# Loading and transposing the first 256 tokens of k and q in another way: sliding-window attention with a gated feed-forward block on one core

## The chip, the core and the metric

The kernel runs on one core of one Trainium2 chip. The time is the device time of one execution in microseconds (us). A core has five engines that run their own instruction streams and wait for each other by semaphores: TensorE (PE in the profile: matmuls and transposes; PEld is its weight load), VectorE (DVE), ScalarE (ACT), GpSimd (POOL) and SyncE (SP). Data moves between the device memory and the on-chip memory (SBUF) by DMA. A DMA is put into a queue by ScalarE or SyncE (the profile calls these queues hardware_dynamic: q10 is ScalarE's, q1 SyncE's) or by GpSimd (software_dynamic, q0). Only DMAs that GpSimd issues change the type on the way here, float32 to bfloat16. TensorE writes into PSUM, eight banks of 2 KB per partition, and VectorE or ScalarE brings results from there to SBUF (an eviction).

## The reference

```python
batch, n_heads, seq, head_dim = (8, 8, 576, 64)
...
scores = scale * np.matmul(q, k.transpose(0, 1, 3, 2))      # scale = 1/8
pos = np.arange(S)
rel = pos[:, None] - pos[None, :]
mask = (rel >= 0) & (rel < 64)
scores = np.where(mask, scores, -1000000000.0)
...
attn = attn / (np.sum(attn, axis=-1, keepdims=True) + 1e-09)   # after the exponential
return np.matmul(attn, v)
...
x = attn_out.transpose(0, 2, 1, 3).reshape(4608, 512)
g = x @ w_gate                                   # 512 x 1536
silu = g * (1.0 / (1.0 + np.exp(-g)))
val = x @ w_val
return silu * val @ w_out                        # 1536 x 512
```

All inputs and the output are float32. q, k and v are [8, 8, 576, 64] (batch, head, token, dimension). Every token sees itself and the 63 before it in its batch.

## The kernel before

The 4608 tokens are cut into 36 chunks of 128 for the attention and 9 blocks of 512 for the feed-forward part. Everything is computed in bfloat16 with float32 sums.

**Attention of a chunk n.** `Sa` takes two PSUM banks, `Sbias` writes the mask into them by two matmuls (identity by `nmask`), `Sb` adds the scores of the 8 heads (24 small matmuls) and ScalarE makes the exponentials into `pt` (two activations, L450). For these the chunk's k and q must lie transposed, the dimension on partitions, in `kT` and `qT`. `AVs` multiplies `pt` by v (`va`, with a column of ones that gives the sum); for n > 0 it reads for half of the rows a copy `vs` in which the last 64 tokens of the chunk before and the first 64 of this one stand together. `shift(n, r, eng)` writes one half of such a copy, on GpSimd or VectorE. `AVn` divides by the sum (a reciprocal and a multiplication on VectorE) and writes `xb`. `X` transposes `xb` into `xT` by TensorE and an eviction.

**Feed-forward.** `F(c, fs, lo, hi)` multiplies the tokens lo to hi of block c by the columns `fs` of both weight matrices (L815), applies tanh on ScalarE and two operations on VectorE, and writes `hT`. `O` multiplies `hT` by the output weights (L850), and ScalarE stores the rows.

**Order.** `build` lists all operations by hand in one sequence; each engine runs those that are its own in that order, and a small graph turns reads and writes of buffers into semaphore waits. An engine that waits holds up everything behind it in its stream. GpSimd is in this way also a queue: a load that it issues can't go out before a `shift` that stands ahead of it. PSUM banks are taken from a written list (`rot`) in the opening and, from `self.lru = True` on, by the one whose last use lies furthest back in the sequence.

**The opening before the change.** `first_loads` brings k of the first 256 tokens as float32 by two hardware DMAs (SyncE, ScalarE), four heads each, on 64 partitions each; a partition holds four tokens of each of the four heads, in rows of 1 KB. They land in `fk`, which borrows space from `hT`. `first_T` casts it on VectorE into `ck` (which borrows from `ost`), then 8 full transposes in two banks and two evictions fill `kT` for chunks 0 and 1. q of these tokens comes by a software DMA (`load2(0, "q")`, two tokens of a head per row) which casts on the way; `T2` transposes it with 16 matmuls of 64 columns in two banks and two evictions. The second 256 tokens of k and q (`load2(1, ...)`) go the same way as this q. `loads` writes the order of GpSimd's queue: the three loads of q and k, then the identity and the mask (selects on GpSimd), then v of four chunks, then the weights in pieces of 256 columns with the shifts between them. `T2w` is a form of `T2` with one bank and one wide eviction, used from the third pair of chunks on. `warm` runs matmuls on zeros into a bank that nobody reads.

Of the kernel before, what the change touches and what calls it, by code (L numbers as in the profile page):

```python
# [9 lines left out]
T = B * S  # L10
# [143 lines left out]
class _Kernel:  # L154
# [17 lines left out]
    def alloc(self):  # L172
# [35 lines left out]
        f4 = lambda a: a.bitcast(F32).rearrange("p (h j d) -> p h j d", h=4, j=4)  # L208
        self.fk = f4(hT[1][:, 0:2048])
        self.fkk = [("hT", 1, f) for f in range(4)]  # L210
        c4 = lambda t: t[:, :].bitcast(BF).rearrange("p (j h d) -> p j h d", j=4, h=4)
        self.ck = c4(self.ost[0])
# [8 lines left out]
    def touched(self, j):  # L221
        k = ("ps", j)
        return max([o.i for o in self.g.readers.get(k, ())] + [o.i for o in self.g.writers.get(k, ())])
# [135 lines left out]
    def T2(self, st, x, engs):  # L359
        g = self.g  # L360
        src = (self.ks2 if x == "k" else self.qs2)[st % 2]
        dst = self.kT if x == "k" else self.qT
        z0 = (2 * st) % self.NZ
        for cc in range(2):
            bank, bk = self.bank("a")
            tb = bank[:, 0:256].bitcast(BF).rearrange("p (c j t) -> p c j t", c=2, j=2)

            def pe(e, cc=cc, tb=tb):
                for c in range(2):
                    for j in range(2):  # L370
                        for p in range(2):
                            r = e.transpose(tb[64 * p:64 * p + 64, c, j, :], src[:, 4 * cc + 2 * c + p, j, :], self.ident[:, :])
                return r

            g.op("pe", pe, reads=["ident", ("s2", x, st % 2, 0), ("s2", x, st % 2, 1)], writes=[bk])
            d = dst[:, 2 * cc:2 * cc + 2, 128 * z0:128 * z0 + 256].rearrange("p c (t j) -> p c t j", j=2)
            a = tb.rearrange("p c j t -> p c t j")
            self.copy(engs[cc], d, a, [bk], [(x + "T", z, cc) for z in (z0, z0 + 1)])

    def T2w(self, st, x):  # L380
# [12 lines left out]

        self.g.op("pe", pe, reads=["ident", ("s2", x, st % 2, 0), ("s2", x, st % 2, 1)], writes=[bk])
        d = dst[:, :, 128 * z0:128 * z0 + 256].rearrange("p c (t j) -> p c t j", j=2)
        a = tb.rearrange("p c j t -> p c t j")
        self.copy("act", d, a, [bk], [(x + "T", z, b) for z in (z0, z0 + 1) for b in range(2)])
# [366 lines left out]
    def first_T(self, engs):  # L764
        g = self.g
        d = self.ck.rearrange("p j h d -> p h j d")
        self.copy("dve", d, self.fk, [("f", 0), ("f", 1)] + self.fkk, [("ost", 0), ("osth", 0)])
        for c in range(2):
            bank, bk = self.bank("a")
            tb = bank[:, 0:256].bitcast(BF).rearrange("p (j t) -> p j t", j=4)  # L770

            def pe(e, c=c, tb=tb):
                for j in range(4):
                    r = e.transpose(tb[:, j, :], self.ck[:, j, 2 * c:2 * c + 2, :], self.ident[:, :])
                return r

            g.op("pe", pe, reads=["ident", ("ost", 0), ("osth", 0)], writes=[bk])
            d = self.kT[:, c:4:2, 0:256].rearrange("p g (t j) -> p g t j", j=4)
            a = tb.rearrange("p j (g t) -> p g t j", g=2)
            self.copy(engs[c], d, a, [bk], [("kT", m, c) for m in (0, 1)])  # L780

    def warm(self, count, n=512, j=None):
        if j is None:
            ids, i = self.rot["a"]
            j = ids[i % len(ids)]
        bank, bk = self.ps[j], ("ps", j)
# [140 lines left out]
    def build(self):  # L927
        F, S, AV, X, T2, O = self.F, self.S, self.AV, self.X, self.T2, self.O
        self.loads()
        self.banks("a", [4, 5, 6, 7, 0, 1, 2, 3, 4, 5, 0, 1, 2, 3, 4, 5, 6, 7, 0, 1, 2, 3, 4, 5, 6, 7, 6, 7])  # L930
        self.warm(72, n=80)
        self.first_T(("dve", "act"))
        s0 = self.Sa(0)
        T2(0, "q", ("act", "dve"))
        self.Sbias(s0)
        self.warm(2)
# [3 lines left out]
        T2(1, "k", ("dve", "act"))  # L940
        T2(1, "q", ("dve", "act"))
        self.early_loads()
        s2, s3 = self.Sa(2), self.Sa(3)
        a0, a1, a2, a3 = self.AVa(0), self.AVa(1), self.AVa(2), self.AVa(3)
        self.AVs(a0)
        self.shift(1, 0, "dve")
        self.AVn(a0)
        self.Sbias(s2)
# [7 lines left out]
        self.warm(1, j=2)  # L956
        self.AVs(a2)
        self.AVn(a2)
        self.AVs(a3)
# [6 lines left out]
        self.banks("a", [4, 5, 6, 7])  # L966
# [3 lines left out]
        self.lru = True  # L970
# [3 lines left out]
        self.T2w(2, "k")  # L974
        self.T2w(2, "q")
# [7 lines left out]
        self.T2w(3, "k")  # L983
        self.T2w(3, "q")
        X(4, "act")
        X(5, "act")
        F(0, (11,))
# [10 lines left out]
        self.T2w(4, "k")  # L998
        self.T2w(4, "q")
# [109 lines left out]
```

## Time and profile before

| | us |
|---|---|
| median of 3 runs | 329.23 (329.14 to 330.06) |
| profiled execution, whole | 330.35 |
| its span, first to last instruction | 328.6 |
| first F matmul (L815) starts | 17.00 |
| TensorE busy in the span | 320.9 (98%) |
| VectorE, ScalarE, GpSimd busy | 214.2, 126.7, 107.2 |

How the times of the opening lie, from the timeline (start and length in us):

| start | length | engine | what |
|---|---|---|---|
| 0.81 | 0.75 | SP | issue of k's first load, lands 5.5 after |
| 0.82 | 0.71 | ACT | issue of k's second load, lands 4.1 after |
| 1.30 | 4.44 | PE | 72 warm-up matmuls |
| 1.32 | 1.01 | POOL | issue of q, first 256 tokens, lands 5.8 after |
| 2.33 | 0.88 | POOL | issue of k, second 256 tokens, lands 6.2 after |
| 3.20 | 0.90 | POOL | issue of q, second 256 tokens, lands 6.9 after |
| 4.16 | 1.13 | POOL | identity and mask, three selects |
| 5.38 | 3.91 | POOL | issue of four loads of v, each lands 5.0 to 5.5 after |
| 6.36 | 0.69 | DVE | cast of k |
| 9.26 | 0.78 | POOL | issue of the first gate weights, land 5.9 after |
| 10.01 | 0.78 | POOL | issue of the first value weights, land 6.5 after |
| 9.20 | 0.4 | PE | scores of chunk 0 |
| 12.79 | 1.3 | PE | scores of chunk 2 |
| 16.14 | 0.9 | PE | A·V of chunks 2 and 3 |

The granted clock of TensorE was 1.00 over the whole span. "Busy" of an engine is the time in which it runs an instruction; TensorE's instructions overlap, so a busy TensorE isn't one at its peak. The landing of a DMA is counted from the start of its issue.

### The profile page before, as it was taken

The page shows a single profiled execution, that of the slowest core. Times are in us where ns is not written, and L with a number is a line of the kernel's source. Part 1 is how long each engine was busy: PE and PEld are TensorE (multiplying, and loading weights), DVE is VectorE, ACT ScalarE, POOL GpSimd, SP SyncE. Part 2 cuts the span into 40 slices and gives each one's busy share as a digit, 9 for nine tenths or more (in the row PEclk, how much of TensorE's full clock was granted, in tenths as well). Part 3 has the DMA queues.
Part 4 walks back from the last instruction along what each step waited for, and adds up shares of the span by engine and source line. Part 5 has one row for each costly group of instructions (what it writes and reads, how often), then busy time and mean ns, then how long its engine had stood idle before and what let it go on. Part 6 is the DMA issues. An engine that isn't in the chain of part 4 may idle for free.

```text
span 328.6 us, 8039 instructions
## 1 busy us (share of the span) xinstructions
PE 320.9 (98%) x3447; PEld 165.7 (50%) x3447; DVE 214.2 (65%) x399; ACT 126.7 (39%) x222; POOL 107.2 (33%) x137
## 2 busy tenths in 40 slices
PE   6899999999999999999999989999999999999996
PEld 6584556475545454545444444545454544444444
DVE  4576954898666767685858586767676767555510
ACT  2645575445433333343324242424242331332221
POOL 8999930582060615050424224241310010000000
PEclk9999999999999999999999999999999999999999
DMA  9999999999999999999796959496939252000012
GB/s 140 178 194 186 196 182 176 154 169 151 132 100 139 127 120 123 135 118 140 116 142 95 153 95 169 87 150 95 158 69 112 67 66 64 34 32 32 34 64 96
DMA packets 157347, 39.33 MB, mean 120 GB/s; under 512 B 144384, under 2 KB 152832, under 8 KB 157312
## 3 DMA queue, kind: packets, MB, share of 16 engines
q0 software_dynamic: 109008, 18.62, 77.9%
q1 hardware_dynamic: 42848, 10.63, 24.5%
q10 hardware_dynamic: 5456, 9.57, 8.7%
q8 instruction: 27, 0.44, 0.6%
q14 instruction: 8, 0.07, 0.1%
HBM read 37.75 MB, written 9.44 MB: 144 GB/s over the span
## 4 chain that ended last, share of the span: by engine, by line
PE 94%; ACT 2%; POOL 1%; issue 1%; DVE 1%; POOLq 0%
PE ps L815 57%; PE ps L850 28%; PE ps L671 3%; PE ps L493 2%; PE ps L438 1%; PE ps L391 1%; PE ps L442 1%; ACT pt L450 1%; PE ps L752 1%; DVE ost L257 1%; POOL qs L332 1%; ACT kT L255 0%; ACT qT L255 0%; PE ps L586 0%; PE ps L418 0%
## 5 line engine op out<-in xcount | busy, mean ns | idle before, releaser
L823 DVE SCALAR_TENSOR_TENSOR uu<-sig,ps 128x512 bf16<-128x512 bf16 x108 | 74.0, 685 | 59.8 <-ACT sig L821 59.5
L815 PE MATMUL ps<-xT,Wg 128*128 128x512 bf16 (+1 forms) x464 | 111.2, 365 | 0.3 <-ACT xT L255 0.3
L815 PE MATMUL ps<-xT,Wv 128*128 128x512 bf16 (+1 forms) x464 | 110.9, 364 | 0.0
L821 ACT ACTIVATE sig<-ps 128x512 bf16<-128x512 f32 x108 | 65.2, 603 | 86.5 <-PE ps L815 86.5
L850 PE MATMUL ps<-Wo,hT 128*128 128x512 bf16 (+1 forms) x444 | 98.5, 373 | 0.0
L323 POOL DMA_DIRECT2D va<-in_v_dram x40 | 34.2, 873 | 143.9 <-PE ps L815 134.5
L825 DVE SCALAR_TENSOR_TENSOR hT<-uu,ps 128x512 bf16<-128x512 bf16 x108 | 74.2, 687 | 3.7
L815 PEld LDWEIGHTS ps<-xT,Wv 128*128 128x128 bf16 x464 | 45.3, 98 | 48.0
L850 PEld LDWEIGHTS ps<-Wo,hT 128*128 128x128 bf16 x444 | 43.3, 98 | 49.5
L815 PEld LDWEIGHTS ps<-xT,Wg 128*128 128x128 bf16 x464 | 43.5, 98 | 44.6 <-ACT xT L255 0.8
L255 ACT ACTIVATE ost<-ps 128x512 f32<-128x512 f32 (+1 forms) x22 | 13.0, 589 | 56.3 <-PE ps L850 56.3
L257 DVE COPY ost<-ps 128x512 f32<-128x512 f32 (+1 forms) x15 | 10.1, 674 | 30.7 <-PE ps L850 30.7
L502 ACT ACTIVATE pt<-ps 128x512 bf16<-128x512 f32 x36 | 18.7, 604 | 29.4 <-PE ps L493 29.4
L323 POOL DMA_DIRECT2D kn<-in_k_dram x29 | 25.9, 905 | 7.0 <-PE ps L815 4.0
L323 POOL DMA_DIRECT2D qn<-in_q_dram x29 | 25.8, 893 | 4.3 <-DMA Wo<-in_moe_w_out_dram 4.3
L450 ACT ACTIVATE pt<-ps 128x512 bf16<-128x512 f32 x36 | 18.7, 604 | 16.5 <-PE ps L442 16.5
L706 DVE TENSOR_TENSOR xb<-ps,rc 128x512 bf16<-128x512 f32 (+2 forms) x48 | 23.1, 510 | 0.6
L671 PE MATMUL ps<-va,pt 64*64 64x65 bf16 x992 | 15.2, 192 | 0.1
L671 PEld LDWEIGHTS ps<-va,pt 64*64 64x64 bf16 x992 | 12.7, 107 | 1.7 <-DVE uu L823 0.4
L702 DVE RECIPROCAL rc<-ps 128x8 f32<-128x8 f32 (+2 forms) x48 | 7.0, 175 | 8.5 <-PE ps L671 8.5
L464 DVE TENSOR_TENSOR pt<-pt,kmask 128x1024 bf16<-128x1024 bf16 x18 | 11.6, 684 | 0.0
L464 DVE TENSOR_TENSOR pt<-pt,mask 128x1024 bf16<-128x1024 bf16 x14 | 9.2, 687 | 0.8 <-ACT pt L450 0.8
(63 smaller groups left out, 125.8 us busy)
## 6 DMA issues: line engine op xcount, KB each, us to landing
out_dram<-ost ACTq DMA_DIRECT2D x35, 256.0 KB, 3.7
va<-in_v_dram POOLq DMA_DIRECT2D x32, 128.0 KB, 5.5
kn<-in_k_dram POOLq DMA_DIRECT2D x23, 128.0 KB, 7.8
qn<-in_q_dram POOLq DMA_DIRECT2D x23, 128.0 KB, 7.8
Wg<-in_moe_w_gate_dram POOLq DMA_DIRECT2D x6, 256.0 KB, 7.4
Wv<-in_moe_w_val_dram POOLq DMA_DIRECT2D x6, 256.0 KB, 7.0
Wo<-in_moe_w_out_dram POOLq DMA_DIRECT2D x2, 768.0 KB, 15.1
qs<-in_q_dram POOLq DMA_DIRECT2D x3, 256.0 KB, 6.9
```

The lines of the kernel that those rows point to most:

```text
L257: self.g.op(eng, lambda e: e.tensor_copy(d, a), reads=reads, writes=writes)
L323: self.g.op("pool", lambda e, d=d, a=a: e.dma_start(d, a), writes=ks, dma=True, after=gate)
L450: g.op("act", lambda e, po=po, p=p: e.activation(po, sv[p], ACTF.Exp, scale=SCALE), reads=[bx[p][1]], writes=[pk[p]])
L464: self.g.op("dve", lambda e: e.tensor_tensor(pt, pt, m, ALU.mult), reads=pk + mk, writes=pk)
L502: g.op("act", lambda e, po=po, p=p: e.activation(po, sv[p], ACTF.Exp, scale=SCALE), reads=[bx[p][1]], writes=[pk[p]])
L671: x = e.matmul(o, ab[0], ab[1], start=first, stop=phase == 1, skip_group_check=True)
L706: g.op("dve", lambda e, av=av, hs=hs, w=w, rc=rc, xo=xo: e.tensor_tensor(xo[:, :, hs, :], av[:, :, :, 0:64], rc[:, :, hs].unsqueeze(3).to_ ...
L815: r = e.matmul(bank[:, a * n:a * n + n], W[:, kk, f * 128:f * 128 + 128], xT[:, kk, lo:hi], start=(kk == 0), stop=(kk == NK - 1))
L821: g.op("act", lambda e, G=bank: e.activation(sig[:, 0:w], G[:, 0:w], ACTF.Tanh, scale=0.5), reads=[bk], writes=[("sig", i)])
L823: g.op("dve", lambda e: e.scalar_tensor_tensor(uu[:, 0:w], sig[:, 0:w], 1.0, G[:, 0:w], ALU.add, ALU.mult), reads=[("sig", i), gk], writes ...
L825: g.op("dve", lambda e: e.scalar_tensor_tensor(out, v3(uu), 0.5, v3(V), ALU.mult, ALU.mult), reads=[("uu", i), vk], writes=[("hT", ih, f) ...
L850: r = e.matmul(OB[:, 0:n], hT[:, f, 128 * u:128 * u + 128], self.Wo[:, f, lo:hi], start=(f == 0), stop=(f == NF - 1))
```

## The change

- `first_loads` now brings k and q by hardware DMAs, two each: even heads by ScalarE, odd heads by SyncE, k ahead of q on both. A partition holds eight tokens of one head: the four heads of a load by 32 groups of eight tokens make 128 partitions, in rows of 2 KB. They land in `hT` (4 KB per partition for each of k and q).
- `first_cast` casts each of the four pieces by itself: k's on VectorE, q's on ScalarE and VectorE. `first_T` makes 8 full transposes into one bank, `first_ev` evicts one chunk of it at a time.
- `T2` is now the one-bank form (the old `T2w`); it gives back a function that evicts the whole of it or one chunk.
- GpSimd's queue begins with the identity and the mask; then v of chunks 0 and 1, the second k and q, v of 2 and 3, and weights and shifts in a new order. `load2(0, "q")` is gone. The copy `shift(1, 0)` moves from VectorE to GpSimd, `shift(3, 0)` from GpSimd to VectorE.
- In `build`, A·V of chunks 0 and 1 stand ahead of the scores of chunks 2 and 3, the masks are written just ahead of each chunk's scores, two short warm-ups are gone, banks are taken by last use from the start, and between 40 and 43 us `F(0, (11,))` and the transposes of the fourth pair's q change places with `X(4)` and `X(5)`.

```diff
@@ alloc
-        self.fk = f4(hT[1][:, 0:2048])
...
+        self.first = {}
+        for i, x in enumerate("kq"):
+            f = hT[1][:, 2048 * i:2048 * i + 2048].bitcast(F32).rearrange("p (e j d) -> p e j d", e=2, j=8)
+            c = self.ost[i][:, :].bitcast(BF).rearrange("p (j e d) -> p j e d", j=8, e=2)
...
@@ T2 (was T2w)
+        def ev(eng, lo=0, hi=2):
+            d = dst[:, :, 128 * (z0 + lo):128 * (z0 + hi)].rearrange("p c (t j) -> p c t j", j=2)
+            self.copy(eng, d, a[:, :, 64 * lo:64 * hi, :], [bk], [(x + "T", z, b) for z in range(z0 + lo, z0 + hi) for b in range(2)])
+
+        return ev
...
     def first_loads(self):
-        for gr, eng in ((0, "sp"), (1, "act")):
-            d = self.fk[64 * gr:64 * gr + 64].rearrange("p h j d -> p h (j d)")
-            a = self.k[0, 4 * gr:4 * gr + 4, 0:256, :].rearrange("h (p j) d -> p h (j d)", j=4)
-            self.g.op(eng, lambda e, d=d, a=a: e.dma_start(d, a), reads=self.fkk, writes=[("f", gr)], dma=True)
+        for x, src in (("k", self.k), ("q", self.q)):
+            f, fkeys, _, _ = self.first[x]
+            for e0, eng in ((0, "act"), (1, "sp")):
+                a = src[0, e0::2, 0:256, :].rearrange("c (g j) d -> c g (j d)", j=8)
+                d = f[:, e0].rearrange("p j d -> p (j d)")
+                self.g.op(eng, lambda e, d=d, a=a: e.dma_start(d, a), reads=fkeys, writes=[("f", x, e0)], dma=True)
+
+    def first_cast(self, x, engs):
+        f, fkeys, c, ckeys = self.first[x]
+        for e0, eng in enumerate(engs):
+            self.copy(eng, c[:, :, e0, :], f[:, e0], [("f", x, e0)] + fkeys, [ckeys[e0]])
+
+    def first_T(self, x):
+        _, _, c, ckeys = self.first[x]
+        bank, bk = self.bank("a")
+        tb = bank.bitcast(BF).rearrange("p (j t) -> p j t", j=8)
+
+        def pe(e):
+            for j in range(8):
+                r = e.transpose(tb[:, j, :], c[:, j, :, :], self.ident[:, :])
+            return r
...
+    def first_ev(self, x, n, eng, b):
+        bank, bk = b
+        dst = self.kT if x == "k" else self.qT
+        a = bank.bitcast(BF).rearrange("p (j c g) -> p c g j", j=8, c=4)[:, :, 16 * n:16 * n + 16, :]
+        d = dst[:, :, 128 * n:128 * n + 128].rearrange("p c (g j) -> p c g j", j=8)
+        self.copy(eng, d, a, [bk], [(x + "T", n, 0), (x + "T", n, 1)])
@@ loads
         self.first_loads()
-        self.load2(0, "q")
-        self.load2(1, "k")
-        self.load2(1, "q")
         self.init()
         self.init_ident()
         self.init_mask()
         self.init_nmask()
-        for n in range(4):
-            self.load(n, "v")
-        self.W(0, 2)
+        self.load(0, "v")
+        self.load(1, "v")
+        self.load2(1, "k")
+        self.load2(1, "q")
+        self.load(2, "v")
+        self.load(3, "v")
+        self.shift(0, 1, "pool")
+        self.load_w("g", 0, 2)
+        self.shift(1, 0, "pool")
+        self.load_w("v", 0, 2)
         self.load_w("g", 2, 4)
-        self.shift(0, 1, "pool")
-        self.load_w("v", 2, 4)
-        self.load_w("g", 4, 6)
         self.shift(1, 1, "pool")
         self.shift(2, 0, "pool")
+        self.load_w("v", 2, 4)
         self.shift(2, 1, "pool")
-        self.shift(3, 0, "pool")
-        self.load_w("v", 4, 6)
+        self.W(4, 6)
         self.W(6, 8)
@@ build
+        self.lru = True
         self.warm(72, n=80)
-        self.first_T(("dve", "act"))
-        s0 = self.Sa(0)
-        T2(0, "q", ("act", "dve"))
-        self.Sbias(s0)
-        self.warm(2)
+        self.first_cast("k", ("dve", "dve"))
+        self.first_cast("q", ("act", "dve"))
+        fk = self.first_T("k")
+        self.first_ev("k", 0, "dve", fk)
+        s0 = self.Sa(0, True)
+        fq = self.first_T("q")
+        self.first_ev("q", 0, "act", fq)
+        self.first_ev("k", 1, "dve", fk)
+        self.first_ev("q", 1, "act", fq)
         self.Sb(s0)
         s1 = self.Sa(1, True)
         self.Sb(s1)
...
+        a0 = self.AVa(0)
+        self.AVs(a0)
+        tk, tq = T2(1, "k"), T2(1, "q")
+        tk("dve", 0, 1)
+        tq("act", 0, 1)
+        tq("act", 1, 2)
+        self.AVn(a0)
+        tk("dve", 1, 2)
         self.early_loads()
...
+        a1 = self.AVa(1)
+        self.AVs(a1)
+        s2 = self.Sa(2, True)
         self.Sb(s2)
-        self.AVs(a1)
         self.AVn(a1)
-        self.Sbias(s3)
+        s3 = self.Sa(3, True)
         self.Sb(s3)
+        self.shift(3, 0, "dve")
         X(0, "dve", "a")
         X(1, "dve", "a")
...
-        self.T2w(3, "k")
-        self.T2w(3, "q")
+        T2(3, "k")("act")
+        F(0, (11,))
         X(4, "act")
         X(5, "act")
-        F(0, (11,))
+        T2(3, "q")("act")
```

More of the change, by code (lines that the diff above doesn't have):

```diff
@@ L207, in alloc @@
         self.ost = ring("ost", self.NO, DM, F32)
-        f4 = lambda a: a.bitcast(F32).rearrange("p (h j d) -> p h j d", h=4, j=4)
-        self.fk = f4(hT[1][:, 0:2048])
-        self.fkk = [("hT", 1, f) for f in range(4)]
-        c4 = lambda t: t[:, :].bitcast(BF).rearrange("p (j h d) -> p j h d", j=4, h=4)
-        self.ck = c4(self.ost[0])
+        self.first = {}
+        for i, x in enumerate("kq"):
+            f = hT[1][:, 2048 * i:2048 * i + 2048].bitcast(F32).rearrange("p (e j d) -> p e j d", e=2, j=8)
+            c = self.ost[i][:, :].bitcast(BF).rearrange("p (j e d) -> p j e d", j=8, e=2)
+            self.first[x] = (f, [("hT", 1, 4 * i + f) for f in range(4)], c, [("ost", i), ("osth", i)])
         self.wup = sb("wup", 1, F32)
@@ L222, in touched @@
         k = ("ps", j)
-        return max([o.i for o in self.g.readers.get(k, ())] + [o.i for o in self.g.writers.get(k, ())])
+        return max([o.i for o in self.g.readers.get(k, ())] + [o.i for o in self.g.writers.get(k, ())], default=-1)
     def bank(self, kind):
@@ L357, in T, with T2 @@
                   writes=[(x + "T", z, 0), (x + "T", z, 1)], dma=True)
[L359 to L380, printed above, removed]
+    def T2(self, st, x):
         src = (self.ks2 if x == "k" else self.qs2)[st % 2]
@@ L758, in first_loads @@
     def first_loads(self):
-        for gr, eng in ((0, "sp"), (1, "act")):
-            d = self.fk[64 * gr:64 * gr + 64].rearrange("p h j d -> p h (j d)")
-            a = self.k[0, 4 * gr:4 * gr + 4, 0:256, :].rearrange("h (p j) d -> p h (j d)", j=4)
-            self.g.op(eng, lambda e, d=d, a=a: e.dma_start(d, a), reads=self.fkk, writes=[("f", gr)], dma=True)
[L764 to L780, printed above, removed]
@@ new lines, in first_T @@
+    def first_T(self, x):
[6 more added lines that the diff above has]
+            return r
+        self.g.op("pe", pe, reads=["ident"] + ckeys, writes=[bk])
+        return bank, bk
+    def first_ev(self, x, n, eng, b):
[4 more added lines that the diff above has]
+        self.copy(eng, d, a, [bk], [(x + "T", n, 0), (x + "T", n, 1)])
@@ L782, in warm @@
     def warm(self, count, n=512, j=None):
[L783 to L786, printed above, removed]
+        bank, bk = (self.ps[j], ("ps", j)) if j is not None else self.bank("a")
         def pe(e):
@@ L939, in build @@
         self.Sb(s1)
-        T2(1, "k", ("dve", "act"))
-        T2(1, "q", ("dve", "act"))
-        self.early_loads()
[L943 to L948, printed above, removed]
+        a0 = self.AVa(0)
[6 more added lines that the diff above has]
+        tk("dve", 1, 2)
+        self.early_loads()
+        a1 = self.AVa(1)
+        self.AVs(a1)
+        s2 = self.Sa(2, True)
         self.Sb(s2)
-        self.AVs(a1)
         self.AVn(a1)
-        self.Sbias(s3)
+        s3 = self.Sa(3, True)
         self.Sb(s3)
+        self.shift(3, 0, "dve")
         X(0, "dve", "a")
         X(1, "dve", "a")
-        self.warm(1, j=2)
+        a2 = self.AVa(2)
         self.AVs(a2)
         self.AVn(a2)
+        a3 = self.AVa(3)
         self.AVs(a3)
@@ L973, in build @@
         F(0, (6,))
-        self.T2w(2, "k")
-        self.T2w(2, "q")
+        T2(2, "k")("act")
+        T2(2, "q")("act")
         self.late_loads()
@@ L997, in build @@
         F(1, (2, 3), 0, 256)
-        self.T2w(4, "k")
-        self.T2w(4, "q")
+        T2(4, "k")("act")
+        T2(4, "q")("act")
         F(1, (4,))
```

4 lines of the change are left out of this document (removed).

## The prediction

> **What bounds the kernel now.** I read the page's slices first, then the chain of waits, then the opening by the timeline and the DMA view.
>
> ```profile
> span 328.6 us, 8039 instructions
> PE   6899999999999999999999989999999999999996
> DMA  9999999999999999999796959496939252000012
> PE 94%; ACT 2%; POOL 1%; issue 1%; DVE 1%; POOLq 0%
> ```
>
> TensorE is full from the second slice (8 us) to the end, and 94% of the chain is its own work. So the change, which touches only the opening and some order up to 55 us, is worth what it moves the start of the first F matmul (L815), if nothing behind it then waits. The chain says where that start is:
>
> ```profile
> 1.32 0.88 POOL qs L332
> ...
> 6.36 0.70 DVE ost L257
> ...
> 7.11 0.62 PE ps L774 x8
> 7.74 0.57 PE ps L372 x16
> ...
> 9.69 2.07 ACT pt L450 x4
> ...
> 13.21 0.74 issue
> ...
> 17.07 1.85 PE ps L815 x16
> ```
>
> First column start, second length. F begins at 17.0 us. Ahead of it lie the cast of k, which ends at 7.06, and about 10 us of transposes, evictions, scores, exponentials and A·V of four chunks. TensorE idles 1.4 us before the first transposes.
>
> The DMA view in small stretches shows who feeds this. q10 is ScalarE's queue, q1 SyncE's, q0 the software queue (packets, MB, share of 16 engines' time); the four fences' lines are of 2 to 3, 4.5 to 4.75, 6.5 to 8, and 316.5 to 319.5 us, one store alone.
>
> ```profile
> q10 hardware_dynamic: 78, 0.08, 58.0%
> ```
> ```profile
> q1 hardware_dynamic: 36, 0.03, 75.0%
> q0 software_dynamic: 60, 0.02, 62.9%
> ```
> ```profile
> q0 software_dynamic: 1072, 0.27, 181.9%
> ```
> ```profile
> q10 hardware_dynamic: 144, 0.26, 23.3%
> ```
>
> Read off: the first row moves some 1.5 us after its issue at 0.82 (2.3 us); the software queue, first issued at 1.32, moves from 4.3, so 3.0 us after issue; alone it moves 180 GB/s (0.27 MB in 1.5 us). The last packet of ScalarE's k load is at about 4.05 and it lands at 0.82+4.1 = 4.92: 0.9 us from last packet to landing. A store is 128 rows of 2 KB plus 16 packets, one closer for each of the 16 engines; 23.3% of 3 us on 16 engines over 144 packets is 78 ns a packet. The k loads have 256+16 packets, so 16 engines too.
>
> **The change part by part.**
>
> *The four loads.* k's two loads of 256 rows of 1 KB become four (k and q, even and odd heads), each 128 rows of 2 KB, 262 KB; q's software load goes (its POOL issue of 1.01 us too). ScalarE and SyncE issue two each at 0.7 us: the second pair goes out at 1.55, ScalarE's table load (1.28 us) moves from 1.56 to about 2.3 and ends by 3.6, ahead of its first use; on SyncE's queue nothing else stands before 50 us. Rows are halved in number, which alone would help. But how many engines carry such a load is shown by no row. In every hardware load and store of the trace, both ends have the partition (64 or 128) as outermost index, and 16 closers show. The new source pattern is heads, groups, tokens: outermost 4, against 128 partitions at the other end. Bounds: 16 engines, as the rows nearest by kind, or 4, one for each outermost source block. I take 4: what all the seen loads have in common, an outermost index of a multiple of 16 at both ends, is just what is given up here, and 4 is the only outermost cut that both ends allow. [...]
>
> *Price on four engines.* Each of the four gets 4 x 32 = 128 rows. A row: 78 ns (the store alone), 84 ns (q10 over the whole execution, 8.7% of 16 x 328.6 us over 5456 packets); above, two 1 KB rows at 62 ns each (64 packets of q1 in 0.25 us on 16 engines) are 124. I take 81, near the two rows of the same size. Alone, 128 x 0.081 = 10.4 us. From about 5.65 us the software queue shares these engines (below). At 4.5 to 4.75 us one hardware queue of 1 KB rows moved 36 KB while the software queue moved 15 KB written, 30 KB read: about equal turns. With two hardware queues I take a third for software: rows 1.5 times as long; bounds 1.0 and 2.0. So 41 rows by 5.65, the other 87 x 0.081 x 1.5 = 10.6 us: last packet 16.2, q lands at **17.1** (13.2 without sharing at 78 ns; 21 at 2.0). k, the first half of each queue, lands at about 9.4.
>
> *From q's landing to F,* by rows: ScalarE cast of half of q 0.6 (128x512 activation, 589 ns); 8 transposes 0.62; two evictions by ScalarE 1.09; four exponentials of chunks 0 and 1, 2.07; ScalarE is free at 4.4 after landing. TensorE ends A·V of chunk 0 at 3.9 and, in order behind it, the second pair's transposes (two of 16) at 4.8; two evictions to 5.9; scores of chunk 2 at 5.75 to 6.2, exponentials of 2 and 3 to 8.3; A·V of chunk 3 0.4. Sum **8.7 us**; F begins at 17.1+8.7 = **25.8**, against 17.0: **+8.8 us**. What lay beside q before (the mask, ident, software loads) is all done by then, so nothing hides it. Idle before q's transposes is about 6 us, longer than any of the trace (1.4 us, at a granted clock of 1.00); what such a pause costs is not shown. About 2 us of the 8.7 are TensorE's own pieces: the bounds are 0 and another 2. I take 0. [...]
>
> *SBUF casts and evictions.* The cast of k (one of 128x1024, 694 ns) becomes two halves, q adds one on VectorE (some 0.35) and one on ScalarE (0.6, counted). Full-array transposes: 8 for q in place of 16 half ones, 0.62 against 0.64. Evictions by chunk, 0.55 to 0.69 each, let chunk 0's scores start one eviction earlier (0.6, counted in the 8.7). The three warm-up matmuls dropped were 0.84 and 0.22 us in gaps.
>
> *POOL's queue.* The three selects (1.2 us) now stand first, from 1.35 to 2.6, then v0, v1, the second pair of k and q, v2, v3 at 0.9 each, so v0 goes out at 2.65 (before 5.38) and moves from 5.65; k of the second pair goes out at 4.45 (before 2.33), q at 5.35 (before 3.20). Then a shift (0.61) stands ahead of each weight load and waits for its v: what is behind it is the weights, and F waits for those. Wg/Wv 0-2 go out at 8.8 and 10.2 or later (9.26 and 10.01 before). With F at 25.8 this is covered: even the four busy engines have 10.4 us of hardware rows and, at 22 GB/s read per engine (180 x 2/16), 8.7 us for their 196 KB of software reads through Wv 0-2: done by 2.3+19.1+0.9 = 22.3. If q landed early that cover would go (second rival).
>
> *Order behind it.* `T2w` renamed costs nothing. Banks by last use from the start: each bank picked was evicted one or more chunks earlier, so cost 0; if a pick were late, one eviction, 0.7. F(0,11) ahead of X(4), X(5): now F(1,(0,1)) waits 0.29 us for the eviction at 42.1 to 43.1; afterwards two evictions, with only k's 1.02 ahead of them, end about 0.35 after TensorE is free. Cost 0, bounds -0.3 and +0.4. VectorE's `shift(3,0)` (0.28) lies beside ScalarE's exponentials.
>
> *Sum.* +8.8 us on the profiled execution, 330.35 us (328.6 of span and 1.75 around it): 339.1. That execution is 1.1 above the median of 329.23, so **338.0 us**. Its own range: 13.2 gives F at 21.9, +4.9, 334; 21 gives F at 29.8, +12.8, 342, and 1 us of the pause's 2 makes 343.
>
> **The rivals.**
>
> 1. *Sixteen engines after all* (or four different ones for each load). Then 1.05 MB move at 290 GB/s (0.29 MB in the third microsecond, 1 KB rows) to 400 (store), in 2.6 to 3.6 us from 2.3, and q lands at 5.8 to 6.8. Now the second pair's q decides: issued at 5.35, landing 6.2 to 6.9 later as before, 11.6 to 12.2; F follows 4.4 later (8.7 less the 4.3 ahead of those transposes), at 16.0 to 16.6, or at 15.4 if its queue is shorter. Gain 0.4 to 1.6, middle 1.0: **328.2**. For it: both ends of every load seen use 16. Against: none of those has such an outermost index. If the 0.74 us stall inside a score block at 13.21 goes away, it is the upper end.
>
> 2. *Sixteen engines, and the weights take over.* A shift waits for each v; Wv 0-2 goes out at 10.2 and lands 6.5 later, 16.7, Wv 2-4 at 12.9+7.0 = 19.9 where F would want it at 18.5. F loses what it gained, or a little more: **329.2**, 328.5 to 330.5. It decides as soon as a v lands 1 us later than its row's 5.5 us.
>
> **How the numbers follow.** Four engines 0.78, rival 1 0.15, rival 2 0.07. The time is the first's, 338.0, its own range 334 to 343, which holds about 0.7. To leave out no more than 0.2 the range has to take in rival 2 and the upper half of rival 1: 328.0 to 343. A difference of 0.3%, 1 us, is about what a measurement of this kernel can tell. Slower by more: 0.78 and a third of rival 2, 0.80; within: the rest of rival 2 and 0.02 of rival 1, 0.07; faster: 0.13.
>
> **What would show it.** Right: the four loads take 4 engines each, so 128 rows and only 4 closers, 132 packets, the DMA's busy share a quarter in the third to sixth microsecond; landing of q's loads 13 to 21 us; idle of TensorE before q's transposes, with the wait on the cast that waits for the load; F at 22 to 30. Wrong: 144 packets a load and q there by 7. If F starts at 16 and the span is not shorter, the weights or a later wait are the cause. If four engines carry it but the software queue hardly slows them, q lands at 13.

## The result, and the profile after

The changed kernel takes 339.23 us (median of 5 runs, 338.87 to 339.78) where the kernel before takes 329.29 beside it (5 runs, 329.14 to 330.8): ratio 1.029, 95% interval 1.0265 to 1.0315. The change costs 9.9 us. The profiled execution took 338.87, with a span of 337.1.

From the page of the changed kernel, the span, three rows of the slices (each digit a tenth of busy time, or of the granted clock, in a fortieth of the span) and the shares of the chain:

```profile
span 337.1 us, 8021 instructions
PE   4299999999999999999999999999999999999996
PEclk9579999999999999999999999999999999999999
DMA  7999999999999999999899999998949161100012
PE 93%; DMA 4%; DVE 1%; ACT 1%; SPq 0%; issue 0%
```

TensorE is full from the third slice on, as it was from the second. A DMA has come into the chain, and the granted clock, 1.00 over the whole span before, has a hole in the first 25 us (0.50 from 8 to 20 us, below). The chain itself, opening only (start, length, what; in the new numbering L761 are the first transposes, L804 is F, L839 is O):

```profile
1.61 14.70 DMA hT<-in_q_dram
...
16.34 0.44 DVE ost L257
...
16.82 1.05 PE ps L761 x8
...
17.89 0.61 ACT qT L255
...
26.28 1.85 PE ps L804 x16
```

q's second load is issued at 1.61 and lands at 16.31; F begins at 26.28 in this chain, where it began at 17.07 in the chain before (the timeline has 26.21 and 17.00). That is 9.21 us. The lag is 9.42 us at F(1,(0,1)) (43.15 before, 52.57 now) and 9.45 at 178 us, so the rest of the program did not make it up and added a quarter of a microsecond. The spans differ by 8.5 only because the profiled execution of before had a wait of its own, near the middle; its chain:

```profile
188.88 0.70 DVE ost L257
189.58 0.76 issue
```

Ahead of this the lag is 9.45, behind it 8.4. That execution took 330.35, 1.1 above the median; this step of about 1.0 fits that. Waits of this kind, for an eviction of O's results by VectorE, stand in the chains of several other versions too, at other places (138 and 189 us with sixteen engines, for one); the one profiled execution of the changed kernel has none.

What the four loads were is in the packets. From 3 to 4 us only ScalarE's queue moves data, and its packets fill a quarter of the time of the 16 engines, so the time of four (packets, MB, share):

```profile
q10 hardware_dynamic: 39, 0.08, 24.9%
```

The DMA queues of the whole execution, changed kernel first, then the one with sixteen engines (the first experiment):

```profile
q1 hardware_dynamic: 42840, 10.89, 22.4%
q10 hardware_dynamic: 5448, 9.83, 8.8%
```
```profile
q1 hardware_dynamic: 42864, 10.89, 23.6%
q10 hardware_dynamic: 5472, 9.83, 9.1%
```

The second fence has 24 packets more on each queue. Each queue carries two of the four loads and nothing else that differs, so that is 12 more a load: 144 against 132 packets, 16 closers against 4. (In the first 20 us with sixteen engines each of these queues shows 288 packets, in the first 45 us of the changed kernel 264, and 0.52 MB both times; a closer is a packet of 4 bytes.) (Before, one load a queue: 42848 and 5456, which is 272 for the load; take it off and add 2 x 132, and the first fence comes out.) So an outermost 4 at the source came with 4 closers and, at 24.9%, the time of four engines.

The clock, in stretches of 2 us (stretch and its length; busy time of PE, PEld, DVE, ACT, POOL; granted clock; DMA share; GB/s):

```profile
6.00:8.00 2.00, 0.00 (x0) 0.00 (x0) 0.17 (x1) 0.00 (x0) 2.00 (x3) 0.97 1.58 180
8.00:10.00 2.00, 0.00 (x0) 0.00 (x0) 0.47 (x1) 0.00 (x0) 0.22 (x1) 0.50 1.60 204
...
18.00:20.00 2.00, 1.46 (x26) 0.64 (x26) 0.00 (x0) 1.73 (x4) 2.00 (x3) 0.50 0.90 99
20.00:22.00 2.00, 2.00 (x67) 1.85 (x68) 0.02 (x1) 1.42 (x3) 1.52 (x4) 0.61 1.47 159
22.00:24.00 2.00, 1.98 (x58) 1.08 (x52) 1.97 (x4) 1.50 (x3) 1.96 (x4) 1.00 1.33 175
```

TensorE has nothing to do from 5.5 to 12.7, the clock falls from 0.97 (mean of 6 to 8) to 0.50 at 8 and is back at 1.00 only shortly before 22. In the chain the eight transposes of q take 1.05 us instead of 0.62.

### The profile page after: what moved, and what is told of

The parts are those of the page before. It is cut to its first block, busy times and chain, and to the rows that moved or that the text cites. A ratio compares the mean times of both kernels' runs of the same rounds, so it can differ in the third digit from the quotient of the medians.

```text
span 337.1 us, 8021 instructions
## 1 busy us (share of the span) xinstructions
PE 322.4 (96%) x3436; PEld 166.9 (49%) x3436; DVE 214.9 (64%) x401; ACT 127.2 (38%) x223; POOL 105.8 (31%) x136
## 3 DMA queue, kind: packets, MB, share of 16 engines
q1 hardware_dynamic: 42840, 10.89, 22.4%
q10 hardware_dynamic: 5448, 9.83, 8.8%
## 4 chain that ended last, share of the span: by engine, by line
PE 93%; DMA 4%; DVE 1%; ACT 1%; SPq 0%; issue 0%
PE ps L804 56%; PE ps L839 28%; DMA hT<-in_q_dram 4%; PE ps L654 3%; PE ps L476 2%; PE ps L421 1%; PE ps L370 1%; PE ps L735 1%; PE ps L425 1%; PE ps L569 0%; DVE xb L588 0%; DVE kT L257 0%; ACT xT L255 0%; PE ps L761 0%; PE ps L401 0%; DVE ost L257 0%
## 5 line engine op out<-in xcount | busy, mean ns | idle before, releaser
L804 PE MATMUL ps<-xT,Wg 128*128 128x512 bf16 (+1 forms) x464 | 111.2, 365 | 0.4 <-ACT xT L255 0.4
L804 PE MATMUL ps<-xT,Wv 128*128 128x512 bf16 (+1 forms) x464 | 110.9, 364 | 0.0
L839 PE MATMUL ps<-Wo,hT 128*128 128x512 bf16 (+1 forms) x444 | 98.5, 373 | 0.0
L810 ACT ACTIVATE sig<-ps 128x512 bf16<-128x512 f32 x108 | 65.0, 602 | 86.2 <-PE ps L804 86.1
L804 PEld LDWEIGHTS ps<-xT,Wv 128*128 128x128 bf16 x464 | 45.4, 98 | 47.9
L839 PEld LDWEIGHTS ps<-Wo,hT 128*128 128x128 bf16 x444 | 43.3, 98 | 49.4
L804 PEld LDWEIGHTS ps<-xT,Wg 128*128 128x128 bf16 x464 | 43.5, 98 | 44.5 <-ACT xT L255 0.5
L323 POOL DMA_DIRECT2D kn<-in_k_dram x29 | 25.4, 884 | 7.0 <-PE ps L804 4.0
L654 PEld LDWEIGHTS ps<-va,pt 64*64 64x64 bf16 x992 | 12.7, 107 | 1.7 <-DVE pt L447 0.4
L761 PE MATMUL ps<-ident,ost 128*128 128x128 bf16 x16 | 2.1, 311 | 9.4 <-DVE ost L257 9.4
## 6 DMA issues: line engine op xcount, KB each, us to landing
Wo<-in_moe_w_out_dram POOLq DMA_DIRECT2D x2, 768.0 KB, 16.8
```

The source lines that it names most:

```text
L323: self.g.op("pool", lambda e, d=d, a=a: e.dma_start(d, a), writes=ks, dma=True, after=gate)
L654: x = e.matmul(o, ab[0], ab[1], start=first, stop=phase == 1, skip_group_check=True)
L804: r = e.matmul(bank[:, a * n:a * n + n], W[:, kk, f * 128:f * 128 + 128], xT[:, kk, lo:hi], start=(kk == 0), stop=(kk == NK - 1))
L810: g.op("act", lambda e, G=bank: e.activation(sig[:, 0:w], G[:, 0:w], ACTF.Tanh, scale=0.5), reads=[bk], writes=[("sig", i)])
L839: r = e.matmul(OB[:, 0:n], hT[:, f, 128 * u:128 * u + 128], self.Wo[:, f, lo:hi], start=(f == 0), stop=(f == NF - 1))
```

## The experiments

### Sixteen, four and two engines

The source of each load is read groups first, heads second, so that its outermost count is 32. In `first_ev` the view is turned to match:

```diff
-                a = src[0, e0::2, 0:256, :].rearrange("c (g j) d -> c g (j d)", j=8)
+                a = src[0, e0::2, 0:256, :].rearrange("c (g j) d -> g c (j d)", j=8)
...
-        a = bank.bitcast(BF).rearrange("p (j c g) -> p c g j", j=8, c=4)[:, :, 16 * n:16 * n + 16, :]
+        a = bank.bitcast(BF).rearrange("p (j g c) -> p c g j", j=8, c=4)[:, :, 16 * n:16 * n + 16, :]
```

> The changed kernel with the four loads' source read in the order groups, heads (outermost 32) in place of heads, groups (outermost 4), the eviction's view turned to match; sizes, rows, queues and everything else as in the changed kernel. Theory (four engines carry a load because its source's outermost index is 4): 144 packets a load, so 272+16 closers... 576 packets for the four instead of 528, q lands at 5.8 to 6.8 us instead of 16.3, F starts at 15.4 to 16.6, time 327.5 to 329.0 (330.35-based sum 328.2). Rival A (what is slow is rows of 2 KB, float32 of q, or the sharing with the software queue): q lands past 12, time above 334. Rival B (16 engines, but the weights behind the shifts take over): q lands by 7, F at 17 or later, time 329 to 330.5.

Measured: 330.49 us (12 runs) beside 330.05 of before, ratio 1.0018 (0.9997 to 1.0039). q's loads were issued at 1.50 and 1.53 and landed 4.8 and 4.1 us later, at 6.3 and 5.6. Its chain, from the second pair's q on:

```profile
5.56 6.03 DMA qs<-in_q_dram
11.63 0.64 PE ps L370 x16
...
16.46 1.85 PE ps L804 x16
```

From 3.5 to 4.0 us the two hardware queues take 94.5 and 10.6% of the time of the 16 engines, so all of them carry these loads. The whole loss is gone with two views turned: same rows of 2 KB, same bytes, same queues, same software traffic. That excludes rival A. F at 16.46 is inside the expected 15.4 to 16.6, and what decides it is the landing of the second pair's q, as thought. But 0.61 us earlier at F did not become 0.5 to 1 less time. In the two profiled executions its lead at the same instructions is 0.45 at 102 us (101.67 against 102.12), 0.31 at 128 and 0.01 at 145 (144.81 against 144.82); between the last two its chain goes through an eviction on VectorE at 138. Its runs spread from 329.7 to 332.3, those of before beside it from 329.1 to 331.5. No difference can be told.

The other way, two heads a load, so eight loads with an outermost count of 2:

```diff
-            for e0, eng in ((0, "act"), (1, "sp")):
-                a = src[0, e0::2, 0:256, :].rearrange("c (g j) d -> c g (j d)", j=8)
-                d = f[:, e0].rearrange("p j d -> p (j d)")
+            for c0 in (0, 2):
+                for e0, eng in ((0, "act"), (1, "sp")):
+                    h0 = e0 + 2 * c0
+                    a = src[0, h0:h0 + 3:2, 0:256, :].rearrange("c (g j) d -> c g (j d)", j=8)
+                    d = f[32 * c0:32 * c0 + 64, e0].rearrange("p j d -> p (j d)")
```

> The changed kernel with each load cut into two of two heads each: eight loads, outermost source index 2, 64 partitions, same rows and same layout in SBUF. Theory: two engines carry all of it, 66 packets a load (64 rows and 2 closers), 256 rows on each of the two instead of 128 on each of four; at the 102 ns a row of the changed kernel (128 rows from 2.4 to 15.4 us) the last packet is at 28.5 and q lands at 29.4; F at 39, time 352 (348 to 356). Rival (the outermost index has nothing to do with it, the order of the heads or the software queue has): as the changed kernel, 339 with at most 2 us for the four more issues.

Measured: 351.42 us in one execution, F at 37.8. Chain of that execution:

```profile
2.83 24.30 DMA hT<-in_q_dram
27.15 0.44 DVE ost L257
```

q lands at 27.1 (expected 29.4). Its two hardware queues have as many packets as the changed kernel's, 42840 and 5448: twice the loads with 64 rows and 2 closers each. The loads take 3.4 and 3.3% of the 16 engines' time in the first 45 us, together 48 us of it; over the 24 us from the first row to the last (0.9 before landing) that is two engines. So q lands at 6.3, 16.3 and 27.1 with 16, 4 and 2 engines: here the count decides, not the rows, the layout or the neighbours. The time per row on the busiest engine, averaged from the first row at 2.3 to 0.9 before landing, is 102 ns on four and 93 on two.

### What the software queue costs these loads

```diff
-        self.load(0, "v")
+        self.load(0, "v", self.q_load)
```

> The changed kernel with the software queue held back: the first load of v, and all behind it, goes out only when q's second load has landed. This asks what sharing the engines with the software queue costs q's loads. By the term in the prediction (81 ns a row alone, 1.5 times as long when shared) q lands at 13.2. Rival (a row takes about 102 ns on these engines whether or not software packets pass, as 39 rows a microsecond on four engines at 3 to 4 us say, before any software packet): q lands at 16, as in the changed kernel. The whole is later in both cases, as v and the second k and q go out some 11 to 13 us later: 342 to 350.

```profile
1.61 12.85 DMA hT<-in_q_dram
```

Measured, from the chain of one execution (343.45 us): q lands at 14.46, between the two expectations. Passing software packets adds 1.85 us to the landing, not 3.5.

From the first row at 2.3 to 0.9 before landing a row takes (14.46 - 0.9 - 2.3)/128 = 88 ns on average, but that average hides two stretches. Up to 5.0 us 87 packets pass on the four engines, 124 ns each, and 83 of them are ScalarE's: SyncE's queue shows its first packet at 4.8, 4.0 us after its issue at 0.81. The changed kernel starts in the same way (90 packets by 5.0, 86 of them ScalarE's). Why SyncE's queue starts so late isn't shown. From 6 to 12 us 304 packets pass here, 156 of SyncE's and 148 of ScalarE's, 79 ns each, close to the 81 of the prediction. The changed kernel moves 121 and 113 in the same six microseconds, 103 ns each. So with the software queue beside it a row takes 1.3 times as long, and once both hardware queues run they take even turns. For the changed kernel from 8 to 12 us:

```profile
q10 hardware_dynamic: 73, 0.15, 12.7%
q1 hardware_dynamic: 74, 0.14, 12.4%
```

### Keeping TensorE warm

Three versions with matmuls on zeros ahead of k's and of q's transposes; the first:

```diff
+        self.warm(110, n=80, j=0)
         fk = self.first_T("k")
...
+        self.warm(44, n=80, j=0)
         fq = self.first_T("q")
```

> The changed kernel with matmuls on zeros while TensorE waits: 110 of 80 columns ahead of k's transposes, 44 ahead of q's. Theory (the granted clock of 0.50 from 8 to 21 us makes TensorE's pieces behind q twice as long, and these are on the chain): clock 1.00 throughout, q's transposes 0.6 instead of 1.05 us, two chunks' mask and scores about 0.9 shorter together; F at 25.0 to 25.4 instead of 26.3, time 0.9 to 1.3 us below the changed kernel, 338.1. Rival (those pieces lie beside ScalarE's exponentials and cost nothing): 339.2, F at 26.3.

Measured: F at 24.91, just under the 25.0 to 25.4 expected, 8.17 us after q's transposes start (16.74) where the changed kernel takes 9.46. But the time is 340.13 (6 runs), ratio 1.0293 (1.0267 to 1.0318): nothing gained. The chain of its profiled execution shows a hole in F:

```profile
86.96 1.88 issue
```

"issue" is time in which TensorE waits for nothing that the profile shows. Up to there the lead over the changed kernel is 1.34 us (its O at 71.03 against 72.37); behind it, it lags by 0.7. The second version has about the same duration in few instructions, 30 and 13 matmuls of 512 columns:

> The changed kernel kept warm again, now by 30 and 13 matmuls of 512 columns in place of 110 and 44 of 80: about as long, with 111 fewer matmuls. With the narrow ones F came 1.37 us earlier but the time did not, and a stall of 1.88 us that no wait explains stood at 87 us. Theory (TensorE ran out of instructions there, because 154 more of them with their weight loads came ahead; with few the stall is gone): F at 24.8 to 25.2 and 1.0 to 1.4 us less time than the changed kernel, a ratio to before of about 1.026. Rival (what is gained by the clock is lost again somewhere whatever it is made of): F at 25, ratio 1.029 to 1.030.

Measured: F at 24.37, again 8.17 us after q's transposes start (16.20, as q landed 0.6 earlier in this execution), but 342.49 us (6 runs), ratio 1.0366 (1.0329 to 1.0402), worse than both expectations. The hole is there again, larger, within the A·V of a chunk:

```profile
83.59 3.29 issue
```

Up to these two points TensorE has 2709 and 2452 records (matmuls and weight loads), 257 apart. Some matmul records are missing from these traces (1349 and 1220 stand there); by the weight loads alone it is 1360 and 1232, 128 apart, so 256 instructions with their matmuls. The third version adds 88 and 40 matmuls of 128 columns, which is 256 records:

> The changed kernel kept warm a third time, by 88 and 40 matmuls of 128 columns: 128 matmuls with their weight loads are 256 instructions. With 308 more instructions TensorE stood still 1.88 us at its record 2709, with 86 more 3.29 us at record 2452, 257 apart, no wait behind either. Theory (TensorE's instructions come in blocks of 256 and the stall is a block that comes late where many small instructions run fast; with 256 more the borders lie in the same places of the program as in the changed kernel, which shows no such stall): no stall over 0.5 us between 80 and 90, F at 24.9, time 1.0 to 1.5 below the changed kernel, ratio to before 1.025. Rival (an earlier F itself brings the stall, by whatever runs at the same time): a stall of 1.5 to 3.5 us again, ratio 1.029 or more.

Measured: no such hole anywhere, 338.57 us (5 runs), ratio 1.0243 (1.0210 to 1.0276), the expected ratio. F came at 25.7, though, not 24.9: the granted clock fell to 0.50 once more, at 20 to 22 (1.00 up to 16, 0.83 from 16 to 20), after pauses that were left, of 1.4 us at 10.7, of 1.0 at 15.4 and of 0.7 at 17.0. So an F some 0.6 us earlier than in the changed kernel came without the hole; the author puts the hole down to where the added instructions put later ones.

That instructions arrive late in blocks of 256 is the author's reading of these two places; the three versions fit it, and the traces show more. The pages count 27 transfers of instructions (queue q8, 0.44 MB, 16 KB each) for the changed kernel and for the second version, and 28 (0.46 MB) for the first and third, which have 308 and 256 instructions more. And such a transfer lies at each of the two holes, first version (86 to 86.25 us) and second (84 to 85):

```profile
q8 instruction: 1, 0.02, 27.8%
```
```profile
q8 instruction: 1, 0.02, 6.8%
```

27.8% of 0.25 us and 6.8% of 1 us on 16 engines are 1.1 us each. The two begin at 86.2 and 84.4 and end at 87.35 and 85.5; TensorE goes on at 88.84 and 86.88, 1.4 to 1.5 us later both times. Before the change a transfer ends at 12.6, and the hole of 0.74 at 13.21 ends 1.3 later. That TensorE waits for these transfers, and why they come when they do, was not tested.

### The rest of the change without its loads

Loads, casts and transposes of the first 256 tokens as before; everything else as changed:

```diff
+        self.load2(0, "q")
...
+        self.first_T(("dve", "act"))
+        s0 = self.Sa(0, True)
+        tq0 = T2(0, "q")
+        tq0("act", 0, 1)
+        tq0("act", 1, 2)
```

> The changed kernel with the loads, the casts and the transposes of the first 256 tokens as they were before (k by the two 64-partition hardware loads in rows of 1 KB, q by the software queue ahead of the selects, 16 half transposes); the new order of weights, v, shifts, A.V and scores, banks, and the order at 40 us stay. Theory (the loss is that of the four loads alone, the rest of the change is worth under 1 us): q of the second pair is issued at about 6.2, lands at 12.2 to 12.5, F at 17.0 to 17.4; time within 1 us of before, 329.0 to 330.5 where before shows 329.3 to 330.0. Rival (the new order itself loses): above 331.

Measured: 330.20 us (12 runs) beside 330.28, ratio 1.000 (0.9983 to 1.0018). The rest of the change is worth nothing either way. F is at 16.66 in the timeline, 0.34 ahead of before, and that meets something the prediction did not name; the waits of TensorE between 40 and 50 us (waiting line, releaser, us in total, times, longest; L830 is O here):

```profile
PE ps L830 <- DMA Wo<-in_moe_w_out_dram: 1.1, 1, 1.1
PE ps L795 <- ACT xT L255: 0.4, 1, 0.4
```

The first O waits for the output weights. Before the change they were issued at 28.8, landed 16.8 later, at 45.6, and the first O began at 45.71.

### Two tries at an earlier F, and one at the output weights

With groups first, the second pair's k and q one place ahead in GpSimd's queue:

```diff
-        self.load(1, "v")
         self.load2(1, "k")
         self.load2(1, "q")
+        self.load(1, "v")
```

> The kernel with sixteen engines (groups first), and in GpSimd's queue the second k and q moved one place ahead, in front of v of chunk 1. With groups first F began at 16.46, 4.83 us after q of the second pair landed (11.59). Theory (this landing is what sets F once q of the first pair is there in time): it lands 0.6 to 0.9 earlier, F at 15.6 to 15.9, and the time is 0.6 to 0.9 below that of groups first. Rival A (TensorE and ScalarE are the bound just behind it): F gains under 0.3. Rival B (an earlier F meets later stalls and gains nothing in the end, as groups first against before): F at 15.6 to 15.9, time the same within 0.3.

Measured: 332.34 us (8 runs), ratio 1.0054 (1.0025 to 1.0083): a loss that none of the three foresaw. The waits of TensorE up to 52 us:

```profile
PE ps L569 <- POOL vs L257: 1.9, 2, 1.0
PE ps L839 <- DMA Wo<-in_moe_w_out_dram: 1.6, 1, 1.6
```

v of chunk 1, now last, lands at 12.19; the shift that needs it holds GpSimd's queue, A·V waits 1.9 us, F begins at 17.46 in the timeline (16.40 with groups first), and every weight goes out later, the output weights among them (second one issued at 30.3).

With groups first, v of chunks 0 and 1 ahead of the selects:

```diff
         self.first_loads()
+        self.load(0, "v")
+        self.load(1, "v")
         self.init()
         self.init_ident()
         self.init_mask()
         self.init_nmask()
-        self.load(0, "v")
-        self.load(1, "v")
```

> The kernel with sixteen engines (groups first), and v of chunks 0 and 1 issued ahead of the identity's and mask's selects, so that GpSimd issues from about 1.3 us instead of waiting for VectorE's fill of the identity until 1.55 and selecting until 2.65; everything behind in its queue goes out about 0.5 us earlier (the second k at 4.2, was 4.70). Theory (F hangs on q of the second pair, and the output weights, which are 0.4 us ahead of their use, come 0.5 earlier as well): F at 15.9 to 16.2 instead of 16.46, no wait on the output weights, time 0.3 to 0.6 below groups first (ratio to before 0.999 to 1.001). Rival (the engines are busy moving anyway, an earlier issue lands no earlier): F within 0.15 of 16.46, time as groups first.

Measured: 330.31 us (12 runs) beside 330.37, ratio 0.9998 (0.9980 to 1.0016). TensorE no longer waits for the second pair's q, but in the profiled execution a hole of 0.77 without a wait, inside chunk 2's scores, takes it back, and F is at 16.76 in the chain (16.46 with groups first). It stands behind 221 weight loads of TensorE; before the change the hole of 0.74 at 13.21 stood behind 222. The time is where it was expected and not below before.

The old loads, and the output weights ahead of the fourth pair's k and q:

```diff
+        self.load_wo(0, 6)
+        self.load_wo(6, 12)
         self.load2(3, "k")
         self.load2(3, "q")
-        self.load_wo(0, 6)
-        self.load_wo(6, 12)
```

> The kernel with the old loads in the changed order (e6), and the two loads of the output weights ahead of the fourth pair's k and q in GpSimd's queue. In e6 TensorE waits 1.1 us at 45 us for the second of them. Theory (these weights come just in time in all these kernels and are the next bound behind F): that wait is gone, nothing takes its place, time 0.8 to 1.1 below e6 (ratio to before 0.997). Rival A (k and q of the fourth pair, which come some 2 to 3 us later, are waited for in their place at 48 to 52 us): time as e6. Rival B (the wait stands beside one that would end as late): as e6, no wait shown.

Measured: 337.15 us (6 runs), ratio 1.0213 (1.0179 to 1.0246). The waits of TensorE, longest first:

```profile
PE ps L370 <- DMA ks<-in_k_dram: 5.0, 1, 5.0
```

The wait on the output weights is gone and one of 5.0 us on k of the fourth pair is in its place: rival A, larger than thought, and earlier (it ends at 45.0). The granted clock is 0.7 in the page's slice of 41.9 to 50.2 us (0.9 or more in all others), and eight F matmuls take 2.79 us behind that wait, from 46.1, where eight took 1.83 at 30.8 before the change. The loads of this part of the program are tight on all sides; no version here beats the kernel before.

## Why the prediction was right

**Four engines.** Right, and shown three ways: 132 packets a load, the loss gone with 16 engines, q's landing 1.8 times as far from the first row with 2. Its reason held in the three versions run: an outermost 32, 4 and 2 at the source came with 16, 4 and 2 engines. That all four loads use the same four engines, on which the 128 rows for each rest, no row of before shows; in the changed kernel the two hardware queues together take 25.1% of the 16 engines' time from 8 to 12 us (12.7 and 12.4), the time of four.

**q's landing,** 17.1 foreseen, 16.3 measured, out of wrong sizes that nearly cancel; that it came so close is luck. The price of a row alone was right: 79 ns measured with both hardware queues running, 81 taken. The start was not: by 5.65 us the sum has 41 rows on each of the four engines, and the trace has 122 packets on all four, some 30 each; SyncE's queue began only at 4.8. The sharing was not either: 1.3 times as long and 1.85 us on the landing, where 1.5 and 3.5 were taken. And the last packet lies 0.4 us ahead of the landing (between 15.9 and 16.0), not 0.9. The rows at 4.5 to 4.75 us, from which a third for software was read, hold a quarter of a microsecond in which one queue was running out; that was too little to take a share from. The even turns of the two hardware queues hold, the common start behind them doesn't, and so k, put at 9.4, came in halves that were cast at 7.8 and 12.2. It cost nothing here, since q is what F hangs on.

**From q to F,** 8.7 foreseen, 10.0 measured (16.31 to 26.28 in the chain). The price of the pause, bounded by 0 and 2 and taken as 0, is the term that was mis-sized. No run shows the 2. What they show: kept warm, in two versions (granted clock 0.91 and 1.00 from 16 to 20 us), TensorE goes from q's transposes to F in 8.17, which with 0.5 of cast is the 8.7; in the changed kernel (0.50 there), in 9.46. So 1.3 us, nearer to the upper bound than to the value taken.

**The sum,** +8.8 foreseen at F, +9.21 measured, which is about what is left of 0.8 too much for q's landing and 1.3 too little behind it; +8.8 on the median, +9.9 measured. The last 0.5 or so of that is not settled: the lag of the two profiled executions is 9.4 and the medians differ by that much and another half.

**Costs put at nothing.** The weights were covered: TensorE waits for none of them in the changed kernel. But the cover was thinner than the sum had it. The software loads were slow beside these four engines' rows as well: v of chunk 0, issued at 2.83, landed 13.7 us later (4.3 with sixteen engines and the same order), the shift ahead of the weights waited for it, and the first weights went out at 17.2 and 18.5, not 8.8 and 10.2. The first value weights landed 6.0 after that, at 24.6, where 22.3 was reckoned, 1.6 us ahead of F. The second pair's q, which the sum has done by the time the first pair's lands, came at 20.2, 14.6 after its issue and some 4 us behind the first's; it cost nothing, as TensorE came to its transposes about 1 us later. The place of X(4) and X(5) costs 0.1 (its wait goes from 0.29 to 0.4). The rest of the change together is nothing within 0.2%, shown by the version with the old loads.

**The rivals.** With 16 engines, F came at 16.46, as rival 1 had it, but its gain of 1.0 us in time did not come. Rival 2 saw that weights would take over, and named the wrong ones: the first weights are in time, the output weights at 45 us were in the kernel before only 0.1 us ahead of their use. "If nothing behind it then waits" was the condition of the whole prediction. It held for the later F of the changed kernel. Where F came earlier or the queue was ordered anew it often did not: 1.1 and 1.6 us of waiting on the output weights in two versions, and with sixteen engines the lead was lost by 145 us, over an eviction at 138.

## What to carry to other kernels

Here loads on a hardware queue whose source had an outermost count of 32, 4 and 2, against 128, 128 and 64 partitions, ran on 16, 4 and 2 engines, and q landed at 6.3, 16.3 and 27.1 us. When rows are made longer by a new order of the source, look at which index now stands outermost and count the closers in the trace (rows and 16, or rows and fewer). In a kernel whose DMA engines are busy throughout, write down for every load when it lands and when it is used before moving any: here a reordering that took 1.1 us of waiting away from one brought 5.0 to its neighbour. And a change at the start of a long unrolled program shifts where later instructions fall: with 308 and 86 instructions added here, TensorE stood still 1.88 and 3.29 us some 70 us later without any wait in the profile; with 256 added no such hole stood there.

## What the runs showed that was not expected

- TensorE stands still without a wait at certain places: 0.74 us behind its 222nd weight load (before), 0.77 behind the 221st (v ahead of the selects), 1.88 behind the 1360th and 3.29 behind the 1232nd (kept warm). The first, the third and the fourth end 1.3 to 1.5 us after a transfer of 16 KB of instructions has ended, and in the version that adds 256 instructions to the changed kernel neither of the last two is there.
- A pause as short as 2.2 us was followed by a granted clock of 0.50, and it came late: in the first warm version TensorE paused from 10.4 to 12.5, the clock was 1.00 at 10 to 12, 0.82 at 12 to 14 and 0.50 at 14 to 16, while TensorE was busy all through these last two microseconds. Before the change a pause of 1.4 us, ahead of the first transposes, went by at 1.00.
- On four engines a 2 KB row from the device memory took 79 ns without the software queue beside it and 103 with it; a 2 KB row of a store on sixteen took 78.
- Two hardware queues whose first loads were issued 0.01 us apart did not start together: on four engines ScalarE's moved from 2.3 and SyncE's from 4.8, 86 packets against 4 by 5.0 us. From there on they took even turns. On sixteen engines the first packets lay 1.1 us apart (2.3 and 3.4).
